# One queue's loads split over two queues, with new orders on all engines, in a fused linear-attention and GEGLU block

## The chip, the cores and the metric

The kernel runs on one core of a Trainium2 chip. The metric is the device time of one execution in microseconds (us); three runs of the kernel before gave 193.61, 193.75 and 194.16, the median being 193.75. All profile rows below come from one profiled execution of that kernel. Its engines are TensorE (PE for matmuls, PEld for weight loads), VectorE (DVE), ScalarE (ACT), GpSimd (POOL) and SyncE (SP). In the profile a "q" behind a name (SPq, ACTq) is that engine's sequencer, which issues DMAs.

## The reference, cut to what matters

Everything is bfloat16, with 2048 rows of 448 features.

```python
x = A_x                                            # [1, 2048, 448]
h = x + attn(layernorm(x))                         # wqkv [448, 1344], wo [448, 448]
#   q, k, v = split(layernorm(x) @ wqkv); 16 heads of 28
#   phi(t) = where(t > 0, t + 1, exp(t)) + 1e-6
#   kv = phi(k)^T v; z = sum over rows of phi(k)
#   o = phi(q) kv / (phi(q) z + 1e-6); attn = o @ wo
g = layernorm(h) @ w_gate                          # [448, 1792]
u = layernorm(h) @ w_up                            # [448, 1792]
h2 = h + (gelu_tanh(g) * u) @ w_down               # w_down [1792, 448]
```

## The kernel before, in words

The rows are cut into 16 tiles of 128, `t` = 0 to 15. A small recorder (`_Graph`) collects 866 tasks with a number and a name each. The engines do not run them in the order in which they were recorded: `ORDERS` holds, for each of PE, ACT, DVE, POOL and SP, the list of task numbers in the order in which that engine issues them. Each engine runs its list strictly in order, and waits on semaphores for results of other engines. A task that waits holds up all that stands behind it on its engine.

The names that the text uses are these.

- Loads: `dx0`, `dx1`, `dx2`, `dx4`, `dx8`, `dx12` (L360) bring x of tile 0, tile 1, tiles 2 and 3, and then four tiles each. `dwq` and `dwk` bring 384 rows of the Q and K weights (L353), `dwq_t` and `dwk_t` the last 64 rows (L356); after the change they are called `dw0`, `dw0_t`, `dw1`, `dw1_t`. `dwg0`, `dwu0` bring columns 0 to 767 of the MLP's gate and up weights, `dwg1`, `dwu1` the rest (L507 to L511). `dwd` brings w_down (L609).
- First layer norm, per tile: `bnst1_t`, `bnag1_t` (DVE, L413, L414), `ln1_t`, `rstd1_t` (ACT, L420, L422). For tiles 0 to 3 `normD_t` (DVE, L435) normalises, PE transposes in two halves `tr0_t`, `tr1_t` (L443), and ACT and DVE copy the halves out (`evxA_t`, `evxD_t`). For tiles 4 to 15 `normP_t` (POOL, L453) normalises and a transposing DMA `xT_t` on SP's queue (L455) turns the tile.
- Projections: `k_t` and `q_t` are four matmuls each (L469). After `k_t` come `ek_t` (ACT), `ck_t` and `pk_t` (DVE), and the sums over rows `pt4_t`, or `pt1_t` and `pt3_t` for later tiles (PE, L488). After `q_t` come `eq_t` and `rq_t` (ACT).
- Middle: `evpD_3`, `z1`, `z0` take the sums out of PSUM; `kv`, `kvm` and `w2_c` fold the value and output weights into one matrix; `evwA_c`, `evwD_c` copy it to SBUF, and `dws0`, `dws1` (SP) copy it between partition halves. For each pair `p` of tiles `cqP_p`, `aqP_p` (DVE), `t1p_t` (POOL), `drP_p`, `rdP_p`, `pnP_p` (DVE) and `deP_p` (ACT) make the normalised q; pairs 0 and 1 have their own forms (`aq_t`, `dr_t`, `deA_t`, `rd_t`, `pn_t`). A transposing DMA `oT_p` (SP, L605) turns it, and `outA_p`, `outB_p` (PE, L627, L628) multiply by the folded matrix. `hr_t` (DVE) adds x.
- Second layer norm: `bnst2_t`, `bnag2_t`; for tiles 0 and 1 `nhD_t` and `wr64_t` (DVE), the PE transposes `trh_t` (L654), and `evhA_0`, `evhD_1`. For the other tiles `negm2`, `vpe2`, `pow2`, `nhP_t` (POOL), `wrap_t` (DVE) and a transposing DMA `hT_t` (SP, L665).
- MLP: five chunks of 2, 2, 4, 4 and 4 tiles. `gu2_v` (two tiles, `v` = 0 to 13) and `gu4_v` (four tiles, `v` = 14 to 55) are the gate and up matmuls (L726, L728). `ge0_v`, `ge1_v` (ACT, L746) apply GELU, `hm0_v`, `hm1_v` (DVE, L748) multiply. Two PSUM bank pairs alternate, so number `v + 2` waits for the `hm` of number `v`. `tbl2` loads ScalarE's GELU table before the first `ge`. `downA_p`, `downB_p` (L696) multiply a pair by w_down, `fo448_t` (DVE, L702) adds h, and `do_t` (SP, L703) stores.

Before, all loads except `dx1`, `dwq_t` and `dwk_t` stand in SP's queue, beside its transposing DMAs; those three stand in ACT's.

Of the kernel before, what the change touches and what calls it, by code (L numbers as in the profile page):

```python
# [12 lines left out]


ORDERS = (
# [33 lines left out]
)  # L49
HOLD = {  # L50
    32: (31,), 35: (34,), 66: (36,), 102: (101,), 127: (126,), 166: (165,), 188: (187,), 214: (213,), 294: (292,),
    305: (302,), 323: (302,), 362: (360,), 388: (387,), 498: (378,), 631: (630,), 707: (704,), 745: (744,), 786:
    (672,), 837: (836,), 864: (863,),
}


# [173 lines left out]
def bass_sequential_preLN__linear_attn_block__glu_gated_geglu__prompt_kernel(  # L230
    nc, A_x, A_wqkv, A_wo, B_x, B_w_gate, B_w_up, B_w_down, out
):
    S, D, FF, H, DH = 2048, 448, 1792, 16, 28
# [14 lines left out]
    G = _Graph()  # L248
    es = ExitStack()
    with es:  # L250
        block = es.enter_context(nc.Block())

        def sb(name, shape, dt):
            return es.enter_context(nc.sbuf_tensor(name, shape, dt))
# [4 lines left out]
        wqk_sb = sb("wqk_sb", [128, 4, 2 * D], BF16)  # L259
        wv_sb = sb("wv_sb", [128, 4, D], BF16)  # L260
        wo_sb = sb("wo_sb", [GW, NG, D], BF16)
        wgu_sb = sb("wgu_sb", [128, NK, FF], BF16)
        wd_sb = sb("wd_sb", [128, NJ, D], BF16)
# [41 lines left out]
        def bufs(name, n):  # L305
            return [_Buf("%s%d" % (name, i)) for i in range(n)]
# [5 lines left out]
        b_wq, b_wk, b_wv = bufs("wq", 2), bufs("wk", 2), bufs("wv", 2)  # L312
        b_wpad = bufs("wpad", 2)
        b_wo, b_wg, b_wu, b_wd = _Buf("wo"), bufs("wg", 2), bufs("wu", 2), _Buf("wd")
# [15 lines left out]
        A_, B_ = slice(0, 64), slice(64, 128)  # L330
# [14 lines left out]
        def dma(q, out_ap, in_ap, w, name, r=(), after=()):  # L345
            t_ = G.add(q, lambda e: e.dma_start(out_ap, in_ap), r=r, w=w, name=name, kind="dma", after=list(after) + last[q])
            last[q] = [t_]
            return t_
# [4 lines left out]
        def dma_w3(q, dst, c0, c1, b, name):  # L353
            return dma(q, dst[:, 0:3, c0 % (2 * D):c0 % (2 * D) + c1 - c0], A_wqkv[0:384, c0:c1].rearrange("(k p) n -> p k n", p=128), [b[0]], name)

        def dma_w1(q, dst, c0, c1, b, name):  # L356
            return dma(q, dst[A_, 3, c0 % (2 * D):c0 % (2 * D) + c1 - c0], A_wqkv[384:448, c0:c1], [b[1]], name)


        def dma_x(q, a, b):  # L360
            return dma(q, x_sb[:, a:b, :], xv[:, a:b, :], b_x[a:b], "dx%d" % a)
# [2 lines left out]
            op("dve", lambda e, dst=dst: e.memset(dst[B_, 3, :], 0.0), [], [b], nm_)  # L364
        dma_x("sp", 0, 1)
        dma_x("act", 1, 2)
        dma_w3("sp", wqk_sb, 0, D, b_wq, "dwq")
        dma_w1("act", wqk_sb, 0, D, b_wq, "dwq_t")
        dma_x("sp", 2, 4)
        dma_w3("sp", wqk_sb, D, 2 * D, b_wk, "dwk")  # L370
        tx1 = dma_w1("act", wqk_sb, D, 2 * D, b_wk, "dwk_t")
        dma_x("sp", 4, 8)
        dma_x("sp", 8, 12)
        dma_x("sp", 12, 16)
# [83 lines left out]
        eks = []  # L458
# [48 lines left out]
        xts = [t for t in G.all if t.name.startswith("xT_")]  # L507
        for i in range(2):
            cs = slice(0, FC) if i == 0 else slice(FC, FF)
            dma("sp", wgu_sb[A_, :, cs], B_w_gate[:, cs].rearrange("(k p) n -> p k n", p=64), [b_wg[i]], "dwg%d" % i, after=xts[-1:])  # L510
            dma("sp", wgu_sb[B_, :, cs], B_w_up[:, cs].rearrange("(k p) n -> p k n", p=64), [b_wu[i]], "dwu%d" % i, after=xts[-1:])  # L511


        op("act", lambda e: e.activation(zbc[B_, :], ps[B_, BK_PT[3], 0:D], AF.Identity), [b_ps[BK_PT[3]]], [b_z[1]], "z1")
# [43 lines left out]
        def a2_pair(p):  # L558
# [3 lines left out]
            if p < 2:  # L562
# [3 lines left out]
                for t in (a, a + 1):  # L566
                    n = t % 2
                    eng = "dve" if t in T1_DVE else "pool"
                    op(eng, lambda e, t=t, n=n: e.tensor_tensor(t1[:, n, :], pq[:, t, :], zbc[:, :], ALU.mult), [b_pq[t]] + b_z, [b_t1[n]], "t1%s_%d" % (eng[0], t))
                for t in (a, a + 1):  # L570
                    n, i = t % 2, t % 4
# [8 lines left out]
            else:  # L580
                i, b2 = 2 * (p % 2), slice(a, a + 2)
# [24 lines left out]
                      r=b_pqn[i2], w=b_pqnT[i2], name="oT_%d" % p, kind="dma")  # L606

            if p == 1:
                dma("sp", wd_sb[:, :, :], B_w_down.rearrange("(j p) n -> p j n", p=128), [b_wd], "dwd", after=[G.all[-1]])  # L609

            if p == 0:
                for n in range(2):
# [139 lines left out]
        for nt in B1_CHUNKS:  # L752
            while done < min(P, (t0 + HR) // 2):
                a2_pair(done)
                done += 1
                if tbl2 is None:
                    tbl2 = G.add("act", lambda e: e.preload_act_table(AF.Gelu_apprx_tanh), name="tbl2", kind="nosync", after=exps)
            gu_chunk(t0, nt)
            for t in range(t0, t0 + nt, 2):
                if t < T - 2:  # L760
                    b2_pair(t // 2)
                else:
                    b2_tile(t)
                    b2_tile(t + 1)
            t0 += nt
# [52 lines left out]
```

## Time and profile before

| what | value |
|---|---|
| median of three runs | 193.75 us |
| profiled execution, its own time | 193.84 us |
| its span on the core | 191.9 us |
| outside the span | 1.94 us |
| PE busy | 185.7 us (97%) |
| DVE busy | 128.4 us (67%) |
| ACT busy | 75.2 us (39%) |
| POOL busy | 50.7 us (26%) |
| granted TensorE clock | 1.00 of full speed throughout |

The span runs from the first to the last record of the program on the core. "Busy" is the time in which an engine executes; issuing a DMA is not counted as busy. Idle time of PE is listed with the instruction that came after it and with what released that instruction.

### The profile page before, as it was taken

How to read it: one execution, taken by the hardware profiler on the slowest of the kernel's cores; microseconds unless marked ns; L12 is line 12 of the kernel's file. 1: busy time of each engine (PE TensorE's matmuls, PEld its weight loads, DVE VectorE, ACT ScalarE, POOL GpSimd, SP SyncE). 2: the span in 40 equal slices, each digit the busy share in tenths (PEclk: the TensorE clock that was granted, in tenths of full speed). 3: DMA queues.
4: the chain of work that ended last, by engine and by line, in shares of the span. 5: the costliest groups of instructions: out<-in, count | busy, mean ns of one | idle time of the engine just before them, and what ended most of it. 6: DMA issues, size and time to landing. Idle time of an engine off the chain costs nothing.

```text
span 191.9 us, 4456 instructions
## 1 busy us (share of the span) xinstructions
PE 185.7 (97%) x1813; PEld 107.3 (56%) x1813; DVE 128.4 (67%) x328; ACT 75.2 (39%) x220; POOL 50.7 (26%) x91
## 2 busy tenths in 40 slices
PE   7899999999899999999999999999998999999994
PEld 7454445655488677886455445444553445455454
DVE  3799879899799998899993863544723244415223
ACT  3689534699954222335132132432320233411200
POOL 6066730525503478235028000006300000000000
DMA  6985647999295505930221520000193000000025
GB/s 171 377 214 76 106 84 168 222 218 192 55 267 135 96 3 101 149 66 3 48 48 35 108 54 0 0 3 2 35 143 67 3 0 0 27 0 24 3 90 173
DMA packets 35077, 17.11 MB, mean 89 GB/s; under 512 B 26865, under 2 KB 33649, under 8 KB 35057
## 3 DMA queue, kind: packets, MB, share of 16 engines
q1 hardware_dynamic: 34752, 16.60, 40.9%
q8 instruction: 14, 0.23, 0.6%
q10 hardware_dynamic: 304, 0.23, 0.4%
q14 instruction: 7, 0.05, 0.1%
HBM read 8.26 MB, written 1.84 MB: 53 GB/s over the span
## 4 chain that ended last, share of the span: by engine, by line
PE 79%; DVE 11%; DMA 4%; ACT 3%; POOL 0%; SPq 0%; issue 0%
PE ps L728 38%; PE ps L696 19%; PE ps L726 7%; PE ps L469 4%; PE ps L488 3%; PE ps L678 3%; PE ps L627 3%; DMA x_sb<-in_A_x_dram 2%; DVE st L413 2%; PE ps L628 2%; DMA xnT<-xnn 2%; DVE pqn L576 1%; DVE den L572 1%; ACT e L480 1%; DVE x_sb L633 1%; DVE w L553 1%
## 5 line engine op out<-in xcount | busy, mean ns | idle before, releaser
L726 PE MATMUL ps<-hnT,wgu_sb 64*128 64x512 bf16 (+1 forms) x490 | 88.8, 333 | 0.7 <-DVE x_sb L702 0.7
L728 PE MATMUL ps<-hnT,wgu_sb 64*128 64x512 bf16 (+1 forms) x490 | 89.0, 333 | 0.0
L746 ACT ACTIVATE gl<-ps 128x256 bf16<-128x256 f32 x112 | 36.4, 383 | 81.8 <-PE ps L726 78.2
L748 DVE TENSOR_TENSOR hh<-ps,gl 128x256 bf16<-128x256 f32 x112 | 42.4, 416 | 38.6 <-ACT gl L746 38.4
L728 PEld LDWEIGHTS ps<-hnT,wgu_sb 64*128 64x128 bf16 x490 | 44.8, 94 | 31.2 <-DVE hh L748 4.6
L726 PEld LDWEIGHTS ps<-hnT,wgu_sb 64*128 64x128 bf16 x490 | 45.0, 94 | 6.3 <-DMA hnT<-hn 1.2
L696 PE MATMUL ps<-wd_sb,hh 64*128 64x448 bf16 x392 | 41.4, 349 | 0.0
L696 PEld LDWEIGHTS ps<-wd_sb,hh 64*128 64x128 bf16 x392 | 21.8, 94 | 15.8 <-issue 0.4
L469 PE MATMUL ps<-wqk_sb,xnT 128*128 128x448 bf16 x128 | 28.2, 355 | 1.0 <-DMA xnT<-xnn 0.4
L413 DVE BATCH_NORM_STATS2 st<-x_sb 128x6 f32<-128x448 bf16 x32 | 19.3, 615 | 3.2 <-DMA x_sb<-in_A_x_dram 3.1
L469 PEld LDWEIGHTS ps<-wqk_sb,xnT 128*128 128x128 bf16 x128 | 11.9, 98 | 12.7 <-DMA xnT<-xnn 1.3
L585 POOL TENSOR_TENSOR t<-pq,zbc 128x448 f32<-128x448 bf16 x12 | 13.0, 1104 | 19.6 <-DVE pq L583 18.1
L488 PE MATMUL ps<-pk,xnn 128*128 128x448 bf16 x64 | 13.9, 353 | 0.0
L627 PE MATMUL ps<-w,pqnT 64*128 64x448 bf16 x49 | 11.5, 349 | 0.8 <-DVE hn L647 0.8
L702 DVE TENSOR_TENSOR x_sb<-ps,x_sb 128x448 bf16<-128x448 f32 x14 | 8.4, 618 | 5.3 <-PE ps L696 5.3
L480 ACT ACTIVATE e<-ps 128x448 bf16<-128x448 f32 x16 | 8.6, 538 | 5.3 <-PE ps L469 5.1
L417 POOL TENSOR_SCALAR nm<-mv 128x1 f32<-128x1 f32 (+1 forms) x19 | 4.0, 218 | 24.3 <-DVE mv L414 24.0
L662 POOL TENSOR_SCALAR hn<-x_sb,nm,rs 128x448 bf16<-128x448 bf16 x14 | 10.3, 745 | 0.5
L628 PE MATMUL ps<-pt_sb,pqnT 64*128 64x448 bf16 x42 | 10.2, 350 | 0.0
L633 DVE TENSOR_TENSOR x_sb<-ps,x_sb 128x448 bf16<-128x448 f32 x16 | 9.7, 614 | 0.8 <-PE ps L628 0.8
L482 DVE SCALAR_TENSOR_TENSOR pk<-ps,e 128x448 bf16<-128x448 f32 x16 | 9.9, 619 | 0.2
L453 POOL TENSOR_SCALAR xnn<-x_sb,nm,rs 128x448 bf16<-128x448 bf16 x12 | 8.9, 743 | 3.5 <-ACT rs L422 2.9
(83 smaller groups left out, 155.5 us busy)
## 6 DMA issues: line engine op xcount, KB each, us to landing
out_dram<-x_sb SPq DMA_DIRECT2D x15, 112.0 KB, 1.8
wd_sb<-in_B_w_down_dram SPq DMA_DIRECT2D x1, 1568.0 KB, 8.0
x_sb<-in_A_x_dram SPq DMA_DIRECT2D x3, 448.0 KB, 6.3
wgu_sb<-in_B_w_gate_dram SPq DMA_DIRECT2D x1, 896.0 KB, 12.2
wgu_sb<-in_B_w_up_dram SPq DMA_DIRECT2D x1, 896.0 KB, 16.5
wqk_sb<-in_A_wqkv_dram SPq DMA_DIRECT2D x2, 336.0 KB, 4.4
wgu_sb<-in_B_w_gate_dram SPq DMA_DIRECT2D x1, 672.0 KB, 6.1
wgu_sb<-in_B_w_up_dram SPq DMA_DIRECT2D x1, 672.0 KB, 8.6
```

The costliest lines, as they stand in the source:

```text
L413: op("dve", lambda e: e.bn_stats(st[:, t, :], src_ap), [b_src], [b_st[t]], "bnst%s_%d" % (tag, t))
L469: ins = e.matmul(ps[:, bk, 0:D], xnT[:, t, k, :], wqk_sb[:, k, c0:c0 + D], start=(k == 0), stop=(k == 3))
L488: ins = e.matmul(ps[:, BK_PT[c], 0:D], xnn[:, t % XN_R, c * 128:(c + 1) * 128], pk[:, ip, :], start=(t == 0), stop=(t == T - 1))
L585: op("pool", lambda e, n=n: e.tensor_tensor(t1[:, n, :], pq[:, a + n, :], zbc[:, :], ALU.mult), [b_pq[a + n]] + b_z, [b_t1[n]], "t1p_%d" % ...
L627: e.matmul(ps[:, BK_OUT[0], 0:D], pqnT[ra, i2, sg // 2, :], w2[ra, sg // 2, :], start=(sg == 0), stop=(sg == 5))
L628: ins = e.matmul(ps[:, BK_OUT[1], 0:D], pqnT[rb, i2, 3 + (sg + 1) // 2, :], (w2 if sg == 6 else w2s)[rb, sg // 2, :], start=(sg == 0), sto ...
L633: op("dve", lambda e, t=t, bo=bo: e.tensor_tensor(x_sb[:, t, :], ps[:, bo, 0:D], x_sb[:, t, :], ALU.add), [b_ps[bo], b_x[t]], [b_x[t]], "h ...
L696: ins = e.matmul(ps[:, BK_O[n], 0:D], hh[rows, j, sl[n]], wd_sb[rows, j, :], start=(half == 0 and j == 0), stop=(half == 1 and j == NJ - 1))
L726: first = e.matmul(psG[:, jj * N:(jj + 1) * N], wgu_sb[A_, k, j * 128:(j + 1) * 128], hnT[A_, ka_, c0:c0 + N], start=(k == 0), stop=(k == ...
L728: ins = e.matmul(psU[:, jj * N:(jj + 1) * N], wgu_sb[B_, k, j * 128:(j + 1) * 128], hnT[B_, kb_, c0:c0 + N], start=(k == 0), stop=(k == NK ...
L746: G.add("act", lambda e, gi=gi, cs_=cs_, psG=psG: e.activation(gl[:, gi, cs_], psG[:, cs_], AF.Gelu_apprx_tanh), r=[b_ps[BK_G[i]]], w=[b_g ...
L748: op("dve", lambda e, dst=dst, srcU=srcU, srcL=srcL: e.tensor_tensor(dst, srcU, srcL, ALU.mult), [b_ps[BK_U[i]], b_glh], [b_ar[j_][t % HR] ...
```

## The change

Two things are changed. First, the queues of some loads. `dx2` (tiles 2 and 3, "three and four" when counted from one) moves ahead of the weights in SP's queue. The 384 rows of Q weights go to ACT's queue, and so do the four gate and up loads and w_down; the condition that put the gate and up loads behind the last `xT` becomes one that puts them behind `ek_11`, and the condition on w_down is dropped. Second, the five lists in `ORDERS` are new, and so is `HOLD` (which of several waits of an instruction is put first). The work itself, its tile sizes, buffers and PSUM banks stay as they were.

```diff
-    "29 35 37 66 46 44 69 53 55 74 79 62 64 82 87 73 90 78 102 86 119 114 94 129 106 165 141 118 133 153 145 177"
...
+    "29 37 35 44 46 66 69 53 74 64 55 79 62 82 87 73 90 78 119 102 86 114 94 129 106 141 165 118 133 153 145 177"
...
         dma_x("sp", 0, 1)
         dma_x("act", 1, 2)
-        dma_w3("sp", wqk_sb, 0, D, b_wq, "dwq")
-        dma_w1("act", wqk_sb, 0, D, b_wq, "dwq_t")
         dma_x("sp", 2, 4)
-        dma_w3("sp", wqk_sb, D, 2 * D, b_wk, "dwk")
-        tx1 = dma_w1("act", wqk_sb, D, 2 * D, b_wk, "dwk_t")
+        dma_w3("act", wqk_sb, 0, D, b_wq, "dw0")
+        dma_w1("act", wqk_sb, 0, D, b_wq, "dw0_t")
+        tx1 = dma_w1("act", wqk_sb, D, 2 * D, b_wk, "dw1_t")
+        dma_w3("sp", wqk_sb, D, 2 * D, b_wk, "dw1")
         dma_x("sp", 4, 8)
...
-            dma("sp", wgu_sb[A_, :, cs], B_w_gate[:, cs].rearrange("(k p) n -> p k n", p=64), [b_wg[i]], "dwg%d" % i, after=xts[-1:])
-            dma("sp", wgu_sb[B_, :, cs], B_w_up[:, cs].rearrange("(k p) n -> p k n", p=64), [b_wu[i]], "dwu%d" % i, after=xts[-1:])
+            dma("act", wgu_sb[A_, :, cs], B_w_gate[:, cs].rearrange("(k p) n -> p k n", p=64), [b_wg[i]], "dwg%d" % i, after=eks[11:12])
+            dma("act", wgu_sb[B_, :, cs], B_w_up[:, cs].rearrange("(k p) n -> p k n", p=64), [b_wu[i]], "dwu%d" % i, after=eks[11:12])
...
-                dma("sp", wd_sb[:, :, :], B_w_down.rearrange("(j p) n -> p j n", p=128), [b_wd], "dwd", after=[G.all[-1]])
+                dma("act", wd_sb[:, :, :], B_w_down.rearrange("(j p) n -> p j n", p=128), [b_wd], "dwd")
```

Read by names, the parts of the new orders that the text uses are these.

| engine | before | after |
|---|---|---|
| SP, start | dx0 dwq dx2 dwk dx4 | dx0 dx2 dw1 dx4 |
| ACT, start | dx1 dwq_t dwk_t tbl1 | dx1 dw0 dw0_t dw1_t tbl1 |
| PE, start | tr0_0 tr1_0 q_0 tr1_1 tr0_1 k_0 | tr1_0 tr0_0 tr0_1 tr1_1 q_0 k_0 |
| SP, first transposes | xT_6 xT_9 xT_7 xT_8 | xT_6 xT_7 xT_9 xT_8 |
| PE | k_6 pt4_4 k_9 k_7 | k_6 pt4_4 k_7 k_9 |
| ACT | ek_11 ek_13 ek_12 ek_14 | ek_11 dwg0 ek_13 dwu0 dwg1 ek_12 ek_14 |
| PE | k_15 ... pt1_15 ... q_4 | q_4 k_15 ... pt1_15 |
| ACT | deA_1 deA_0 ... deA_2 | deA_0 dwu1 deA_1 deA_2 |
| DVE | evpD_3 z0 aq_1 t1d_0 | aq_1 evpD_3 z0 t1d_0 |
| DVE | nhD_1 cqP_3 wr64_1 wr64_0 rdP_2 | nhD_1 rdP_2 wr64_0 wr64_1 ... cqP_3 |
| ACT | evhA_0 eq_14 rq_12 eq_12 tbl2 | evhA_0 rq_15 eq_13 rq_14 eq_14 rq_13 tbl2 |
| ACT | ge0_1 ge1_2 | ge0_1 deP_3 dwd ge0_2 |
| SP | dws0 dws1 oT_1 oT_2 dwd oT_3 hT_2 hT_3 | dws0 dws1 oT_1 oT_2 oT_3 hT_3 hT_2 |
| PE | outB_3 downA_0 gu2_7 gu2_8 | outB_3 gu2_7 gu2_8 downA_0 |
| POOL | nhP_4 ... nhP_7 t1p_11 t1p_10 | t1p_11 t1p_10 ... nhP_5 nhP_4 ... nhP_7 |
| SP, last four tiles | hT_14 do_3 hT_15 do_4 hT_12 hT_13 | hT_13 do_3 hT_15 hT_14 hT_12 |
| PE, end | downA_6 down448_14 downB_6 down224_15 (two) | downA_6 down224_15 downB_6 down448_14 down224_15 |

More of the change, by code (lines that the diff above doesn't have):

```diff
@@ L15 @@
 ORDERS = (
[33 rows of a table removed]
[34 rows of a table added]
 )
 HOLD = {
-    32: (31,), 35: (34,), 66: (36,), 102: (101,), 127: (126,), 166: (165,), 188: (187,), 214: (213,), 294: (292,),
-    305: (302,), 323: (302,), 362: (360,), 388: (387,), 498: (378,), 631: (630,), 707: (704,), 745: (744,), 786:
-    (672,), 837: (836,), 864: (863,),
+    66: (36,), 139: (138,), 165: (164,), 175: (174,), 305: (298,), 362: (360,), 388: (387,), 431: (283,), 498:
+    (375,), 521: (518,), 531: (528,), 571: (570,), 581: (580,), 591: (590,), 621: (620,), 699: (497,), 755:
+    (754,), 767: (764,), 849: (846,), 864: (863,),
 }
```

65 rows, old and new, of the table ORDERS are left out of this document.

## Prediction

> **What bounds the kernel now.** I read the page's busy shares first, then stretches of the span, the waits of PE's weight loads, the chain, and the DMA views.
>
> ```profile
> PE 185.7 (97%) x1813; PEld 107.3 (56%) x1813; DVE 128.4 (67%) x328; ACT 75.2 (39%) x220; POOL 50.7 (26%) x91
> ```
>
> TensorE sets the time, and the change removes none of its 1813 matmuls. Only its idle time can be won, or added to. Stretches of the span (start:end, length, PE, PEld, DVE, ACT, POOL busy, clock, DMA share, GB/s) show where that idle time is:
>
> ```profile
> 0.00:7.90 7.90, 6.23 (x52) 5.09 (x53) 3.71 (x11) 3.05 (x9) 3.06 (x10) 1.00 0.78 250
> ...
> 34.10:49.00 14.90, 14.14 (x92) 7.71 (x90) 14.36 (x36) 13.40 (x35) 6.26 (x8) 1.00 1.05 202
> 49.00:52.20 3.20, 3.15 (x34) 1.77 (x36) 2.35 (x4) 2.81 (x7) 2.39 (x2) 1.00 0.08 15
> 52.20:145.50 93.30, 93.30 (x1094) 57.22 (x1090) 67.74 (x169) 30.09 (x92) 27.47 (x44) 1.00 0.38 71
> 145.50:146.30 0.80, 0.08 (x3) 0.04 (x4) 0.70 (x2) 0.00 (x0) 0.00 (x0) 1.00 0.19 39
> ```
>
> From 52.2 to 145.5 PE never stops, so a stall put there is lost in full. Between 34.1 and 49.0 VectorE is busy for 14.36 of 14.90 us: it sets that stretch. The waits of the weight loads (total, times, longest) name what PE lacks:
>
> ```profile
> PEld ps L469 <- DMA xnT<-xnn: 1.3, 2, 0.8
> PEld ps L627 <- DMA pqnT<-pqn: 1.3, 1, 1.3
> PEld ps L726 <- DMA hnT<-hn: 1.2, 1, 1.2
> ```
>
> All are transposing DMAs of SP's queue. In starts of matmuls the losses are 0.18 and 0.57 us at `k_6` and `k_7` (18.38, 21.23), 0.98 at `outA_1` (49.05) and 0.88 at 146.27. The chain shows the first loss of all, tiles 2 and 3 of x, and the second:
>
> ```profile
> 1.71 4.70 DMA x_sb<-in_A_x_dram
> ...
> 6.43 0.63 DVE st L413
> ...
> 17.77 3.41 DMA xnT<-xnn
> ...
> 21.23 0.93 PE ps L469 x4
> ```
>
> A DMA's time runs from issue to landing. In the stretch 43 to 46 us the issues read:
>
> ```profile
> pt_sb<-w SPq DMA_DIRECT2D x1, 168.0 KB, 5.4
> pqnT<-pqn SPq DMA_TRANSPOSE x1, 5.2
> ```
>
> That `oT_1` landed at 49.0; the seven of its kind have a median of 2.9. It stood behind the MLP weights in one queue (the last issued at 30.9, 16.5 to land).
>
> **Start.** `dx2` is issued at 1.24 instead of 1.71, without 336 KB of Q weights ahead of it. Its landing is bounded by the same flight of 4.70 (5.94, from 6.41) and by about 4.1 (the first tile lands at 3.3; 224 KB more at some 300 GB/s). The Q weights now share the engines with it, so I take 5.1. VectorE is free of tile 1 at 5.15 (`bnag1_1` 5.06, then 0.09), so `bnst1_2` goes from 6.43 to about 5.2. But `k_0` needs the K weights, which landed at 7.3 with the same bytes to move ahead of them. Thus `k_0` goes from 7.92 to 7.45: 0.45 us. ScalarE issues one more load before `tbl1` (2.43): some 0.5 us, the table ends at 4.2, just where `ln1_0` (4.19) needs it. Cost 0, or 0.1 if the issue is slow.
>
> **Projections.** All first transposes begin 0.5 us earlier and `xT_7` goes ahead of `xT_9`, so the losses of 0.75 at `k_6`, `k_7` should go. VectorE, never idle from 7.9 to 21.2 (13.30 of 13.30), is late next; I leave 0.3 for waits on `pk_4` to `pk_6`, so 0.45 is won.
>
> Three gate and up issues now stand in ScalarE's list between `ek_11` and `ek_12`. At 0.63 to 0.69 each that is 2.0 us, beside six operations of 0.43: 4.6 us against 5.3 us of matmuls from `k_13` to `k_15`. Cost 0, but `ek_13` and `pk_13` wait behind them if ScalarE is late. `dwg0` goes out near 26.5, while `xT_15` (27.6 before) is near 26.6: they collide. Before, `dwg0` needed over 1.5 us from issue to any dense traffic, so I take 0.2, up to 1.0.
>
> **Middle.** From `evpD_3` (34.13) to the end of `wr64_0` (49.00) VectorE's strip is 14.87 us. `aq_1` (0.39) and `cqP_3` (0.35) leave it, `rdP_2` (0.26) enters: 14.4. `dwu1` (0.69) stands between `deA_0` and `deA_1` on ScalarE, with `rd_1` and `pn_1` waiting behind; the new order uses them 2 us later, so 0, at most 0.7. The strip starts after `pt1_15`, which now has `q_4` (0.76) ahead of it: 34.13 + 0.76 - 0.45 - 0.45 + 0.2 = 34.2. So `wr64_0` ends at 48.6 to 49.3. `outA_1` no longer waits for `oT_1`, as weights and transposes are in different queues, so `trh_0` follows `wr64_0` directly instead of at 49.92. The first MLP matmul (52.14) comes 1.2 us earlier; bounds 0.4 and 1.8 (all waits gone).
>
> Here the Trainium skill speaks against the change: "DMA: Bandwidth & Descriptors", section "Issuing engines are not separate DMA queues", says that issuing from several engines saves only issue time. By it `oT_1` would still be late; that is the second rival below. No run yet decides it.
>
> **Into the MLP.** Between `evhA_0` and `tbl2` ScalarE has five `eq`/`rq` instead of three: 0.86 us. `ge` of `gu2_0`, then `hm1_0`, move back as much, and `gu2_2` had about 0.4 us of cover after the last `hm` (55.68 to 55.95, plus latency). A new loss of 0.4, from 0 to 0.6.
>
> `dwd` moves from 52.02 to behind `deP_3`, about 4.3 us after the first MLP matmul. Its issue (0.58) stands before `ge0_2`, where ScalarE idled 1.42: 0. It is needed by `downA_0`, now about 16 us after that matmul, and took 8.0 to land: covered by 4. But its 8 us now lie on `oT_3`, `hT_3`, `hT_2`, which it preceded before. Alone these need 2.9 to 3.1 each; their packets move 229 KB at about 215 GB/s, 1.07 us each. Bounds: nothing (they slip between the weights), or all three behind the whole load: 4.3 + 8.0 + 3.2 = 15.5 against a need by `gu2_7` at 65.48 - 52.14 = 13.3, 2.2 us. `outA_3` has 1.6 us of cover for `oT_3`. I take 0.6, nearer to nothing: `oT_3` has most of its cover used before `outA_3` waits, and the weights' traffic starts thin, as `dwg0`'s did.
>
> **Late MLP.** The stall at 146.27 came from SP's queue (start, length, count):
>
> ```profile
> 137.13 1.22 SPq L665 DMA_TRANSPOSE hnT<-hn  x1
> 138.40 0.58 SPq L703 DMA_DIRECT2D out_dram<-x_sb  x1
> 139.02 1.23 SPq L665 DMA_TRANSPOSE hnT<-hn  x1
> 140.29 0.58 SPq L703 DMA_DIRECT2D out_dram<-x_sb  x1
> 140.92 3.62 SPq L665 DMA_TRANSPOSE hnT<-hn  x2
> ```
>
> One store (0.63 with its gap) leaves, and the first transpose follows the first `wrap` (136.2) instead of the third: 0.9 earlier. Together 1.5, over 0.88, so the stall goes: 0.88 won, 0.5 if a transpose is again 1 us late. POOL's two `t1p` (1.04 each) now precede `nhP_4` to `nhP_7`; `hT_5` should still land over 1 us before its matmul: 0, or 1.0 if that cover is gone. Stores move to the end of SP's list, 0.48 apart; the last still follows `fo224_15` (189.37): 0, or 0.5 if one is in its way. All other reorderings keep two matmul groups between a bank's use and reuse: 0.
>
> **Sum**, on the profiled execution (193.84; 0.09 over the median): 193.84 - 1.2 + 0.4 + 0.6 - 0.88 = 192.76, or 192.7 against the median. What this kernel can tell from no change is about 0.3%, 0.6 us.
>
> **Rivals.** *Two queues collide* (slower). Weights from ScalarE's queue alternate with the transposes on the same DMA engines, so that a transpose takes as long as the weights beside it. Price: 2.2 instead of 0.6 at `gu2_7`, and 0.8 more at `xT_15`: 192.7 + 1.6 + 0.8 = 195.1. It decides once the collisions cost 1.7 us (0.6 + 1.1). For it: the two tiles of x that were issued at 0.8 on two queues landed after 2.5 and 2.7, so neither queue goes first. Against: `oT_3` has 1.6 us of cover. The skill ("DMA: Bandwidth & Descriptors", "Queues, rings and completion order") states that each DMA engine goes round-robin between its queues, a packet at a time; the trace agrees with its 2.5 and 2.7.
>
> *VectorE hides the start.* If the strip and the dense stretch before it set the first MLP matmul, it comes only 0.2 earlier: with half of the costs 193.84 - 0.2 + 0.3 + 0.3 - 0.88 = 193.4, no measurable change. For it: VectorE's 14.36 of 14.90. This is also the result if `oT_1` stays late on its own queue.
>
> *All cover holds.* 193.75 - 1.8 - 0.88 = 191.1. For it: each cost has cover by its nearest row; against: that all do.
>
> That the change does not do what it says is not a rival of weight: the loads do move.
>
> **Numbers.** Forecast 0.40 (0.35 faster, 0.05 same), all cover 0.09 (faster), hidden 0.16 (0.03 faster, 0.10 same, 0.03 slower), collision 0.35 (0.01 same, 0.34 slower). So faster 0.47, same 0.16, slower 0.37. The forecast's own range is 191.9 to 193.5, from its bounds. The 8-in-10 range reaches nearly to full cover and just over the collision: 191.4 to 195.2.
>
> **What would show it.** Right: the first MLP matmul near 51; no PEld wait on pqnT at L627; `bnst1_2` near 5.2; no gap before the last chunk's first matmul. Collision: PEld waits at L726 or L627 on hnT or pqnT between 58 and 68, or on xnT near 30, with transposes at 4 us or more from issue to landing. Hidden: first MLP matmul at 51.9 or later. The forecast is wrong if PE waits over 1 us on VectorE or ScalarE in a place not named here.

## The result, and the profile after

The kernel after takes 196.25 us (median) against 193.75 us before: a ratio of 1.014, with a 95% interval of 1.011 to 1.017. It is slower by 1.4%. Of six runs five took 195.91 to 197.51 us and give the ratio; the sixth took 201.24 at a lower granted clock and is left out of it. Its profiled execution took 196.05 us with a span of 194.3, against 193.84 and 191.9 before; the forecast was 192.7.

The first line of the page (busy time, share of the span and instructions of each engine) shows that the work of TensorE is what it was:

```profile
PE 185.2 (95%) x1813; PEld 115.4 (59%) x1813; DVE 127.9 (66%) x328; ACT 76.1 (39%) x220; POOL 49.6 (26%) x91
```

PE is busy for nearly the same time (185.2 us against 185.7) and its share fell from 97% to 95%, so the 2.4 us by which the span grew are new idle time. Cut into stretches where the trace's matmuls stop (columns as in the prediction: PE, PEld, DVE, ACT, POOL busy, clock, DMA share, GB/s), the span shows two holes:

```profile
0.00:7.25 7.25, 5.52 (x52) 4.58 (x53) 4.52 (x15) 3.48 (x10) 2.68 (x10) 1.00 0.75 245
30.60:34.00 3.40, 1.26 (x8) 0.51 (x6) 1.71 (x4) 1.22 (x3) 0.00 (x0) 1.00 1.23 188
36.76:50.90 14.14, 14.14 (x96) 7.62 (x94) 13.97 (x35) 12.19 (x32) 5.52 (x5) 1.00 0.75 158
...
63.90:66.20 2.30, 0.33 (x7) 0.10 (x4) 2.30 (x7) 0.66 (x2) 0.97 (x1) 1.00 1.12 104
66.20:148.90 82.70, 82.53 (x911) 56.16 (x912) 54.83 (x139) 24.54 (x76) 21.88 (x36) 1.00 0.32 52
```

`k_0` starts at the end of the first row. The second row holds a stop ahead of `k_15`. The third is VectorE's strip from `evpD_3` to `wr64_0`: 14.14 us, with PE now busy in all of it. The fourth is a stop ahead of `outA_3`, inside the stretch where PE never stopped before. Taken by starts of matmuls, as in the prediction, the stops are 2.30 and 2.13 us. The chain of waits (start, length, what) names what ended each of them; these are its lines around the first and the second:

```profile
26.30 0.91 POOL xnn L454
...
27.24 6.34 DMA xnT<-xnn
33.59 0.14 issue
33.73 0.92 PE ps L470 x4
```

```profile
59.55 6.44 DMA pqnT<-pqn
66.00 0.14 issue
66.13 0.35 PE ps L628
```

Both are transposing DMAs on SP's queue, `xT_15` and `oT_3`. Before, they took 2.4 and 2.9 us from issue to landing; now 6.34 and 6.44. What moved in the meantime can be read from the DMA queues. q10 carries what ScalarE issued (the loads), q1 what SP issued (`xT_15` has packets of 256 bytes). The columns are packets, MB and the share of 16 engines' time. First the stretch 28.5 to 30.5 us, then 31 to 32.5 us:

```profile
q10 hardware_dynamic: 270, 0.41, 84.5%
```

```profile
q1 hardware_dynamic: 516, 0.13, 93.3%
q10 hardware_dynamic: 98, 0.13, 65.8%
```

`xT_15` was issued from 27.24 to 28.43. In two microseconds after that not one of its packets moved; `dwg0`, issued at 26.33 on the other queue, had the engines to itself. `xT_15` moved once `dwg0` had nearly gone: by 31 us 372 of the 448 packets of `dwg0` had moved. `oT_3`, issued from 59.55 to 60.78, shows the same behind `dwd`: from 58 to 62 us only q10 moved.

```profile
q10 hardware_dynamic: 1365, 1.22, 94.9%
```

So the places and the culprits are those of the rival *two queues collide*. Its 2.2 us for `dwd` was the price of waiting for the whole load, and 2.13 were measured. For `xT_15` it had 1.0 us (0.2 and 0.8 more); there, too, the wait was for nearly the whole load, 2.30.

### The profile page after: what moved, and what is told of

Same layout as the page of the kernel before. It is cut to its first block, busy times and chain, and to the rows that moved or that the text cites. A ratio compares the mean times of both kernels' runs of the same rounds, so it can differ in the third digit from the quotient of the medians.

```text
span 194.3 us, 4464 instructions
## 1 busy us (share of the span) xinstructions
PE 185.2 (95%) x1813; PEld 115.4 (59%) x1813; DVE 127.9 (66%) x328; ACT 76.1 (39%) x220; POOL 49.6 (26%) x91
## 3 DMA queue, kind: packets, MB, share of 16 engines
q1 hardware_dynamic: 30688, 11.44, 29.5%
## 4 chain that ended last, share of the span: by engine, by line
PE 80%; DMA 11%; DVE 4%; issue 1%; ACT 1%; ACTq 1%; POOL 1%
PE ps L729 31%; PE ps L697 17%; PE ps L727 9%; PE ps L470 9%; DMA xnT<-xnn 5%; PE ps L489 4%; DMA pqnT<-pqn 3%; DMA wqk_sb<-in_A_wqkv_dram 3%; PE ps L679 3%; PE ps L628 3%; PE ps L629 2%; DVE hh L749 1%; PE ps L618 1%; ACTq L347 1%; PE ps L548 1%
## 5 line engine op out<-in xcount | busy, mean ns | idle before, releaser
L727 PEld LDWEIGHTS ps<-hnT,wgu_sb 64*128 64x128 bf16 x490 | 45.4, 94 | 2.3
L697 PEld LDWEIGHTS ps<-wd_sb,hh 64*128 64x128 bf16 x392 | 23.0, 94 | 14.3 <-issue 0.2
L470 PEld LDWEIGHTS ps<-wqk_sb,xnT 128*128 128x128 bf16 x128 | 11.9, 98 | 14.4 <-DVE pk L483 2.5
L586 POOL TENSOR_TENSOR t<-pq,zbc 128x448 f32<-128x448 bf16 x12 | 12.3, 1040 | 28.3 <-DVE pq L584 25.9
L489 PEld LDWEIGHTS ps<-pk,xnn 128*128 128x128 bf16 x64 | 6.3, 98 | 5.8 <-DVE pk L483 0.2
```

The lines of the kernel that those rows point to most:

```text
L470: ins = e.matmul(ps[:, bk, 0:D], xnT[:, t, k, :], wqk_sb[:, k, c0:c0 + D], start=(k == 0), stop=(k == 3))
L489: ins = e.matmul(ps[:, BK_PT[c], 0:D], xnn[:, t % XN_R, c * 128:(c + 1) * 128], pk[:, ip, :], start=(t == 0), stop=(t == T - 1))
L586: op("pool", lambda e, n=n: e.tensor_tensor(t1[:, n, :], pq[:, a + n, :], zbc[:, :], ALU.mult), [b_pq[a + n]] + b_z, [b_t1[n]], "t1p_%d" % ...
L697: ins = e.matmul(ps[:, BK_O[n], 0:D], hh[rows, j, sl[n]], wd_sb[rows, j, :], start=(half == 0 and j == 0), stop=(half == 1 and j == NJ - 1))
L727: first = e.matmul(psG[:, jj * N:(jj + 1) * N], wgu_sb[A_, k, j * 128:(j + 1) * 128], hnT[A_, ka_, c0:c0 + N], start=(k == 0), stop=(k == ...
```

## The experiments

All times below are for the kernel after with one edit, unless another base is named. Each was taken beside the kernel before on the same chip, and the ratios are to that. The median of the kernel before was 193.11 to 193.23 us there, some 0.5 below the 193.75 of the result, so times are best compared with each other and not with 196.25. "One run" marks a time that was measured once. "Gap" is PE's lost time between two starts of matmuls.

The main theory, *order of issue*: DMAs of both queues are served in the order in which they were issued. The rivals: *shares* (the queues alternate packet by packet, the prediction's own mechanism), *turns* (whole loads alternate), *yields* (a transpose gives way to any plain load).

**A second load ahead of `xT_15`.** In ScalarE's order:

```diff
-ek_11 dwg0 ek_13 dwu0 dwg1 ek_12
+ek_11 dwg0 dwu0 ek_13 dwg1 ek_12
```

> Only the place of dwu0 changes: ScalarE issues it right behind dwg0 (about 27.0), ahead of xT_15 (27.24); in the kernel after it came behind xT_15 (27.85). Theory, order of issue: DMAs of both queues are served in the order in which they were issued, so xT_15 waits for both loads. dwu0's traffic takes about 3.9 us more (landings of dwg0 and dwu0 in the kernel after: 33.08 and 36.99), so xT_15 lands near 37.3 instead of 33.59, k_15 waits some 6.0 instead of 2.3 us, and the time is about 199.7. Rival, turns: the queues are served by turns, one whole DMA each; xT_15 comes behind dwg0 alone as before, lands near 33.6, gap 2.3, time 196.0. Rival, shares (the prediction's own mechanism): the queues alternate packet by packet; one more load behind the first in ScalarE's queue takes no larger share, so also near 33.6 and 196.0.

Measured: 204.92 us (one run). PE's waits (total, times, longest) and the stretches around `k_15` (its start is 39.97):

```profile
PE ps L471 <- DMA xnT<-xnn: 8.5, 2, 8.0
```

```profile
38.00:39.90 1.90, 0.00 (x0) 0.00 (x0) 0.00 (x0) 0.00 (x0) 0.00 (x0) 0.50 0.70 138
39.90:42.00 2.10, 2.04 (x6) 0.87 (x7) 0.00 (x0) 0.35 (x1) 0.00 (x0) 0.50 0.40 98
42.00:44.00 2.00, 2.00 (x6) 0.73 (x5) 1.20 (x3) 0.63 (x2) 0.00 (x0) 0.50 0.03 6
```

`k_15` waited 8.2 us, so *turns* falls: `xT_15` came behind both loads. *Shares* as stated falls with it. Two things went beyond the expected 6.0. `dwg1` was issued from 28.18 to 28.78, inside the issue of `xT_15` (27.58 to 28.95), and the two then went packet for packet. The queues from 36 to 38 us:

```profile
q10 hardware_dynamic: 128, 0.26, 95.7%
q1 hardware_dynamic: 127, 0.03, 14.2%
```

And the clock granted to TensorE (the column before the DMA share) was 0.50 after the stop: until 45.4 us a matmul of 448 columns took 0.374 us instead of 0.19. The span is 8.9 us longer than that of the kernel after. The longer stop is 5.9 of them, and 5.4 us at half speed lose another 2.7, by an estimate from these rows.

**The loads behind `xT_15`.**

```diff
-ek_11 dwg0 ek_13 dwu0 dwg1 ek_12
+ek_11 ek_13 dwg0 dwu0 dwg1 ek_12
```

> dwg0, dwu0 and dwg1 are issued behind ek_13, so dwg0 near 27.85, 0.6 us after xT_15 (27.24); all stay on ScalarE's queue, dwu1 stays where it is. Theory, order of issue: xT_15 lands after its usual 2.4 to 2.7 us (29.7 to 30.0), k_15 starts near 31.4 without a gap, and 2.3 us are won there. But everything behind then comes 2.3 earlier while the loads come a little later: dwu1 lands near 47.5, oT_1 (issued near 43.5) waits for it and lands near 49.5, and outA_1, wanted near 47.8, gives back 1.5 to 2.2. Time 195.3 (194.8 to 196.0). Rival, shares: dwg0 and xT_15 overlap for over 1 us of traffic, xT_15 needs 4 us or more, k_15 keeps a gap near 0 (its cover is 4.2 us from issue), and oT_1 is slowed little: 193.8. Rival, transposes yield to any plain load: xT_15 waits for dwg0 again, lands near 34.5, gap 3, time 196.7.

Measured: 194.24 us, ratio 1.006 (1.004 to 1.008). `xT_15` was issued at 27.64 and landed after 2.4 us; `k_15` had no gap. The queues from 28.5 to 29.5 us and from 29.9 to 31.5 us:

```profile
q1 hardware_dynamic: 511, 0.13, 62.8%
```

```profile
q10 hardware_dynamic: 198, 0.30, 80.1%
```

`dwg0`, issued 0.6 us behind `xT_15`, began when the transpose was through. That contradicts *yields*. As expected, part of the gain was given back later:

```profile
PE ps L629 <- DMA pqnT<-pqn: 2.2, 2, 1.6
```

`oT_1` (issued at 43.88) landed at 48.71, behind `dwu1`, which landed at 47.13, and `outA_1` had a gap of 0.72. It was less than the 1.5 to 2.2 expected, as `oT_1` landed 0.8 earlier than the 49.5 put down for it. `oT_3`, still behind `dwd`, cost 1.76.

**`dwd` ahead of the GELU table.** In ScalarE's order, from behind `deP_3`:

```diff
-rq_15 eq_13 rq_14 ... deP_3 dwd ge0_2
+rq_15 dwd eq_13 rq_14 ... deP_3 ge0_2
```

> Only the place of dwd in ScalarE's order changes: behind rq_15, issued near 52.4, just behind oT_2 (52.02), instead of 56.64. Theory, order of issue: dwd lands near 59.6, before oT_3 (issued 59.55) has any traffic, so oT_3 lands after its usual 2.9 us (62.5), the gap of 2.13 at outA_3 goes, and the time is 194.0 (193.8 to 194.4, the upper end if the issue delays the first GELUs). oT_2 keeps its landing. Rival: the gap at outA_3 only stands in for one that is due anyway behind it (hT_3, hT_2 and VectorE's work for gu2_7), so that gu2_7 then waits over 1 us, and the time stays over 195.

Measured: 200.45 us, ratio 1.037 (1.033 to 1.041), against an expected 194.0. The expectation assumed an issue at 52.4. The timelines of ScalarE's and of SyncE's sequencer (start, length, what) show another order:

```profile
50.60 0.38 ACTq L348 DMA_DIRECT2D wd_sb<-in_B_w_down_dram  x1
```

```profile
51.05 1.22 SPq L607 DMA_TRANSPOSE pqnT<-pqn  x1
```

The load does not wait until the activation ahead of it in the list has begun: `rq_15` began to execute at 51.41. So the list is the order in which ScalarE's sequencer issues, and not the order in which the work begins. Here `dwd` was ahead of `oT_2` by 0.45 us, `oT_2` took 8.7 us, and the stop moved to `outA_2`:

```profile
PEld ps L629 <- DMA pqnT<-pqn: 4.6, 1, 4.6
```

```profile
60.00:62.00 2.00, 2.00 (x16) 1.02 (x14) 0.00 (x0) 0.00 (x0) 0.00 (x0) 0.50 0.50 94
62.00:64.00 2.00, 2.00 (x23) 1.35 (x21) 0.00 (x0) 0.00 (x0) 0.00 (x0) 0.50 0.00 0
```

`outA_3` had no gap. The expected time was missed, but the wait went where the theory puts it, to the transpose that now stood behind the load. Again the clock was 0.50 after the stop of 4.48.

The same edit was made again, with `dwd` behind `rq_14` and one more condition, so that it is surely behind `oT_2`:

```diff
+        G.dep(by["dwd"], [by["evhD_1"]])
```

> Only dwd is moved in the kernel after, as in wd_early, but it is issued only once evhD_1 is done and so surely behind oT_2, whose issue begins near 52.0. Theory, order of issue: oT_2 lands after its usual 2.9 to 3.2 us, dwd (issued near 52.9) lands near 60.3, oT_3 (59.55) near 62.6, and both gaps, 4.48 at outA_2 in wd_early and 2.13 at outA_3 in the kernel after, are gone: 194.0 (193.8 to 194.4). Rival, transposes wait for any plain load under way or about to start: oT_2 waits again, over 198.

Measured: 192.96 us (one run). `oT_2` took 3.0 us and `oT_3` 2.9, neither `outA_2` nor `outA_3` had a gap, and `k_15` still had one of 1.44 behind `dwg0`. The time is 1.0 less than the 194.0 expected; that smaller gap is 0.86 of it, and the other chip can be a part. The gap at `outA_3` was a real loss, and no later stop stood behind it.

**`dwd` between `oT_3` and `hT_3`.**

```diff
-ge0_1 deP_3 dwd ge0_2 ge1_2 ge0_3 ge1_3 ge1_4
+ge0_1 deP_3 ge0_2 ge1_2 ge0_3 ge1_3 dwd ge1_4
```

> Only the place of dwd in ScalarE's order changes: behind ge1_3, issued near 60.8, after oT_3 (59.55) and just ahead of hT_3 (61.10) and hT_2. Theory, order of issue: oT_3 lands after its usual 2.9 us (62.5) and the gap at outA_3 goes, though the same load is under way beside it; hT_3 and hT_2 wait for the whole load (landing near 68), land near 69.5 and 70.5, and gu2_7, wanted near 66.9, waits some 3.7 us. Time 197.6. Rival, shares: oT_3 is a little slower, hT_3 and hT_2 take 4 to 5 us, land at 65 to 66, and gu2_7 does not wait: 194.0 to 194.5.

Measured: 198.71 us (one run). The DMA issues from 60 us on, with their time to landing, in which the first two rows are `dwd`, and `hT_3` and `hT_2`:

```profile
wd_sb<-in_B_w_down_dram ACTq DMA_DIRECT2D x1, 1568.0 KB, 9.1
hnT<-hn SPq DMA_TRANSPOSE x2, 8.4
```

`oT_3`, issued at 59.04, 0.94 ahead of `dwd`, landed after 3.02 us; `hT_3`, issued 0.6 behind it, after 8.7. `gu2_7` waited 3.64 (expected 3.7). The transposes are the same kind on the same queue; only their place in the order of issue differs. *Shares* had 194.0 to 194.5. The 1.1 us over the expected 197.6 fits the clock, which was 0.50 from 71.18 to 74.59 us: 3.4 us at half speed lose 1.7, and the gap at `k_15` was 0.8 smaller than in the kernel after.

**All five loads back on SP, the rest of the change kept.** This undoes the queue change of the MLP loads alone and puts them back in their places of the kernel before:

```diff
-            dma("act", wgu_sb[A_, ...], ..., "dwg%d" % i, after=eks[11:12])
-            dma("act", wgu_sb[B_, ...], ..., "dwu%d" % i, after=eks[11:12])
+            dma("sp", wgu_sb[A_, ...], ..., "dwg%d" % i)
+            dma("sp", wgu_sb[B_, ...], ..., "dwu%d" % i)
...
-                dma("act", wd_sb[:, :, :], ..., "dwd")
+                dma("sp", wd_sb[:, :, :], ..., "dwd")
```

> The kernel after, with its start and its orders, but all five MLP loads back on SyncE's queue at the places of the kernel before: dwg0, dwu0, dwg1, dwu1 behind xT_15, dwd between oT_2 and oT_3. Theory, order of issue: it is the time of issue and not the queue that counts. xT_15 lands after 2.4 us (2.3 won), oT_3 after 2.9 (2.1 won); dwu1 lands near 47, so oT_1 (issued near 43.7) waits for it and outA_1 has a gap of 0.7 to 1.3: 196.05 - 2.3 - 2.1 + 1.0 = 192.6, ratio 0.994 (0.990 to 0.998). So this undoes the whole loss and shows what the rest of the change is worth. Rival, a second queue helps by itself: moving the loads back costs what the prediction had put down to it (oT_1 behind the weights, 1.2 us of the middle, and more at outA_1), and the time is 194 or over, no faster than the kernel before.

Measured: 192.45 us, ratio 0.9965 (0.994 to 0.999). `k_15` and `outA_3` had no gap, `outA_1` one of 1.05, since `oT_1` (43.57) stood behind `dwu1` and landed at 48.71. So the whole loss lies in the MLP loads, and the rest of the change is worth 0.7 us (0.3 to 1.1 by the interval). `oT_1` landed at the same 48.71 in *the loads behind `xT_15`*, with the loads on the other queue: the queue made no difference.

**`dwu1` and `dwd` behind their transposes, on ScalarE's queue.** The edit of *the loads behind `xT_15`*, and:

```diff
+        G.dep(by["dwu1"], [by["cqP_2"]])
+        G.dep(by["dwd"], [by["evhD_1"]])
```

with `dwu1` behind `rq_11` and `dwd` behind `rq_14`.

> Every MLP load is issued just behind a transpose that would otherwise wait for it, all still on ScalarE's queue: dwg0, dwu0, dwg1 behind ek_13 (as in gu_late), dwu1 behind rq_11 and not before cqP_2 is done (so behind oT_1), dwd behind rq_14 and not before evhD_1 is done (so behind oT_2). Theory, order of issue: xT_15, oT_1, oT_2 and oT_3 all land 2.4 to 3.2 us after issue, and the two gaps that gu_late's profile still had, 0.72 at outA_1 and 1.76 at outA_3, go: gu_late's ratio to before, 1.0059, less 2.5 of 193.2 us gives 0.993 (0.989 to 0.996), about 1.4 us faster than the kernel before. Rival, VectorE's strip sets the middle: outA_1's gap goes but the first MLP matmul does not come earlier, only outA_3's is won: ratio 0.997. Rival, shares: transposes that overlap the loads still take 4 us or more; ratio 1.00 or above.

Measured: 198.71 us, ratio 1.028 (1.025 to 1.031). A miss. The chain and the issues show `oT_1`:

```profile
44.40 9.26 DMA pqnT<-pqn
```

```profile
44.40 1.35 SPq L607 DMA_TRANSPOSE pqnT<-pqn  x1
```

```profile
44.62 0.60 ACTq L348 DMA_DIRECT2D wgu_sb<-in_B_w_up_dram  x1
```

`dwu1` began 0.22 behind `oT_1`, but its issue was complete at 45.22 and that of `oT_1` at 45.74. Now both were in service together. From 48 to 49.5 us the packets went one for one:

```profile
q10 hardware_dynamic: 119, 0.24, 88.0%
q1 hardware_dynamic: 118, 0.03, 16.8%
```

`outA_1` waited 5.13 us, with the half clock behind it. So "issued first" has to be sharpened. Where a load did not disturb the transpose ahead of it, the issue of the transpose had also *ended* first (`dwg0` and `xT_15` of *the loads behind `xT_15`*: 28.89 and 28.83, `dwd` and `oT_3` of *`dwd` between*: 60.36 and 60.27). Here, as with `dwg1` and `xT_15` of *a second load*, the load began later and ended earlier, and the two shared the engines.

The test of that keeps ScalarE's queue and lets `dwu1` wait a little longer:

```diff
-        G.dep(by["dwu1"], [by["cqP_2"]])
+        G.dep(by["dwu1"], [by["hr_0"]])
```

> As both_late, all MLP loads on ScalarE's queue, but dwu1 is issued only once hr_0 is done, so that its issue ends after that of oT_1 (in both_late it ended 0.52 us before). Theory, order by the end of issue: oT_1 lands after 2.5 to 3.2 us instead of 9.26, outA_1's gap of 5.13 and the half clock behind it go, and the time is that of sp_behind within 0.5 us, though the loads are on the other queue. Rival: a second queue is what lets a load disturb a transpose that was issued first; oT_1 stays at 5 us or more, outA_1 has a gap of over 2 us, and the time is over 195.

Measured: 191.89 us (one run). The issues, SyncE's and ScalarE's:

```profile
43.41 1.35 SPq L607 DMA_TRANSPOSE pqnT<-pqn  x1
```

```profile
44.82 0.60 ACTq L348 DMA_DIRECT2D wgu_sb<-in_B_w_up_dram  x1
```

1.41 us behind instead of 0.22, and `oT_1` took 3.3 us instead of 9.26; `outA_1` had no gap. The load was issued 1.2 us later on the same two queues, and the time is 6.8 us less (198.71 against 191.89, on two chips): about the stop of 5.13 and the 1.7 that 3.4 us at half clock lose by estimate.

Is it the end of the issue that decides, or a lead of some 0.6 us between the beginnings? Every undisturbed transpose of the runs had both. But in *a second load* `dwg1` began 0.60 us behind `xT_15`, as far as `dwg0` did in *the loads behind `xT_15`* (0.60) and `dwu0` in the kernel after (0.60). These two ended 0.06 and 0.03 behind the transpose and did not disturb it; `dwg1` ended 0.17 ahead of it and shared the engines with it. So the same lead came out both ways, and the order of the ends tells them apart. It is one case, and in it two loads were already ahead.

**The same with the loads on SP**, that is the kernel with all five loads on SP and `dwu1` behind `oT_1` in its list:

```diff
-dwg0 dwu0 dwg1 dwu1 dws0 dws1 oT_1 oT_2 dwd oT_3
+dwg0 dwu0 dwg1 dws0 dws1 oT_1 dwu1 oT_2 dwd oT_3
```

> As mlp_on_sp, with dwu1 moved from behind dwg1 to behind oT_1 in SyncE's list, so that its issue begins only when oT_1's has ended. Theory, order by the end of issue (a load waits for a transpose and a transpose for a load, whichever had been issued completely first, whatever the queue): dws0, dws1 and oT_1 land 2.3 to 3 us after issue, the gap of 1.05 at outA_1 goes, and the next task, trh_0, then waits for wr64_0 of VectorE, done 0.95 before trh_0's present start: 0.95 us faster than mlp_on_sp, 0.9965 less 0.0049 = 0.992 of before (0.989 to 0.995). oT_2 (issued near 48.8, with dwu1 still moving until 50) lands 1 to 2 us late, within the cover of outA_2. Rival: loads beside a transpose slow it however they are ordered, as oT_1's 9.3 us beside dwu1 in both_late might mean; then outA_1's gap is 3 us or more and the ratio 1.005 or above.

Measured: 191.37 us, ratio 0.992 (0.989 to 0.995), as expected. Its gap at `outA_1` is gone, `trh_0` waits 0.14 for VectorE, and from 52 to 146 us PE is nearly back to what it was before (93.80 us busy of 94.00):

```profile
52.00:146.00 94.00, 93.80 (x1096) 65.26 (x1093) 66.81 (x169) 30.77 (x93) 28.71 (x45) 1.00 0.39 69
```

This version is faster than both kernels, by 0.8% against before. The single run with the loads on ScalarE's queue lies 0.5 us above it.

**`dw1_t` ahead of `dx4`.** In the early loads, on the kernel just shown (a separate run of the edit on the 198.71 us kernel gave the same picture, see below):

```diff
-        tx1 = dma_w1("act", wqk_sb, D, 2 * D, b_wk, "dw1_t")
         dma_w3("sp", wqk_sb, D, 2 * D, b_wk, "dw1")
+        dma_w1("sp", wqk_sb, D, 2 * D, b_wk, "dw1_t")
```

> As sp_behind, with dw1_t on SyncE's queue ahead of dx4, as in both_late_k, where k_0's last quarter no longer waited. Theory: the stall of some 0.4 to 0.7 us in k_0 goes, dw1_t lands near 7.3: 0.4 to 0.5 us faster than sp_behind, ratio 0.989 (0.986 to 0.993). Rival: VectorE, which has no idle time from 8 to 21 us, takes the gain back before k_10, and the ratio stays that of sp_behind.

Measured: 191.76 us, ratio 0.993 (0.990 to 0.996): no gain that can be told from its base, so the rival's outcome. The step itself worked: `dw1_t` landed at 7.61, and `k_0` had no gap, where its base had 0.61. But `q_0` had one of 0.39 and `k_6` one of 0.36, which the base had not, and the base had one of 1.01 at `k_9`. Stops at these places differ from run to run (`q_0` from none to 0.95 and `k_9` from none to 1.01 in kernels that have the same loads there), and a gain of 0.4 cannot be told apart in that. Whether VectorE takes it back stays open. On the 198.71 us kernel:

> As both_late, and dw1_t (the last 64 rows of the K weights) is issued on SyncE's queue between dw1 and dx4, near 2.17 instead of behind dx4's issue at 2.31 on ScalarE's; ScalarE issues one load less before its table load. Theory, order of issue, at the start too: dw1_t lands near 7.3 instead of 8.2 to 8.8, as it no longer stands behind dx4's 448 KB, and the stall of 0.2 to 0.6 in k_0's last quarter goes: 0.4 us faster than both_late, ratio 0.991. Rival: the small loads land late for their own small packets and not for their place; k_0's stall stays and the ratio is that of both_late.

Measured: 198.26 us, ratio 1.026 (1.023 to 1.030), with `dw1_t` at 7.33 and no gap in `k_0`. The two intervals overlap, so the 0.45 us there is not shown either.

## Why the prediction was wrong

**The start** was right in its steps. `dx2` landed at 4.79 (forecast 5.1), `bnst1_2` started at 5.12 (5.2), `k_0` at 7.27 (7.45). What was missing is a row I did not price: `dw1_t`, the last 64 rows of the K weights, was issued behind `dx4`, landed at 8.20, and stopped `k_0` for 0.41 before its last quarter.

**Projections**: half right. `k_6` and `k_7` lost nothing, but `k_9` lost 0.55 to `xT_9`, so that `k_11` came 0.41 earlier, where 0.9 had been forecast together with the start. The issues of loads cost ScalarE nothing, as forecast.

**The step that failed: `xT_15` against `dwg0`**, "I take 0.2, up to 1.0". It was 2.30. The reason given, that `dwg0` needed over 1.5 us to any dense traffic, is true (few packets before 29 us) and beside the point: the transpose did not move in the thin part either. The bound of 1.0 allowed for two loads that share the engines; the runs show a wait for all of the earlier one.

**The middle**: the strip was right (14.14 us against 14.4). The number behind it seems to fit too: the first MLP matmul was 1.04 later than before, and so 1.26 earlier without the 2.30, where 1.2 was forecast. That is luck, since the reason "as weights and transposes are in different queues" is refuted. `oT_1` was early because `k_15`'s stop had given the loads 2.3 us. With that stop away and ScalarE's queue kept (*the loads behind `xT_15`*), `outA_1` lost 0.72 and the first MLP matmul started at 51.84, only 0.30 earlier than before; on SP's queue `outA_1` lost 1.05. The section "Issuing engines are not separate DMA queues" of the Trainium skill's page "DMA: Bandwidth & Descriptors" says that issuing from several engines saves only issue time. The runs agree: `oT_1` landed at 48.71 from either queue.

**Into the MLP**: the `eq` and `rq` cost 0.21 at `gu2_2` (0.4 forecast, from 0 to 0.6). **The second step that failed is `dwd`**, 0.6 with a bound of 2.2. It was 2.13, and at `outA_3`, not at `gu2_7`: `oT_3` was 3.5 us late against its 1.6 us of cover, which was named correctly. The upper bound was the case that occurred; the choice "nearer to nothing" rested on the same thin traffic.

**Late MLP**: right. No gap ahead of the last chunk's first matmul, 0.88 won, and no store in the way at the end.

With the two measured stops in the place of 0.2 and 0.6 the sum gives 192.76 - 0.8 + 2.30 + 2.13 = 196.39, against 196.05. All other terms together were off by 0.3 us. That is closer than they deserve: projections won less than forecast, and the 1.2 of the middle holds only together with the stop at `k_15`.

**The rivals**: *two queues collide* named the places and got 195.1. Its mechanism, an alternation, is only part of the truth. The Trainium skill ("DMA: Bandwidth & Descriptors", "Queues, rings and completion order") has each DMA engine go round the queues that it has work for, a packet at a time. The trace agrees where two DMAs are in service together (119 packets against 118). Where one had been issued well before, the trace shows no turns: 270 packets against none. Whether `xT_15` was then held back at the DMA engines or had not been handed to them yet, no run shows. An alternation from the issue on, as the rival had it, would have moved packets of `xT_15` from 28.5 us on.

## What to carry to other kernels

In this kernel a small DMA that an engine waits for was late by all the bytes that had been issued ahead of it, on whichever queue. That holds for the plain copies too: `dws0` and `dws1` took 4.7 to 5.5 us from issue to landing where most of `dwu1` was still ahead of them, on either queue, and 2.6 to 2.9 where `dwu1` was issued after them. Moving a big load to another engine's queue did not take it out of the way, and put it in the way, because its issue was no longer ordered against the small one. Issue each big load right behind the small transfer that would otherwise wait for it, in the same list or with an explicit condition that comes clearly later, and check the issue times of both in the trace. When a load is moved, price the wait of every short transfer that is issued before the load lands at the load's full remaining time first, and lower it only with a row that shows the two moving together.

## What the runs showed of the hardware that was not expected

- Service across the two queues followed the order of issue. A transpose issued less than 1 us behind a load took 5.5 to 8.7 us, behind two loads (and beside a third) 12.3, and just ahead of one, with its issue ended first, 2.4 to 3.3. What in the hardware keeps this order, no run shows.
- A transpose and a load that began later but whose issue ended first went packet for packet, and both became slow: `oT_1` took 9.26 and `dwu1` 9.2 us, where they took 3.3 and 7.2 with `dwu1` issued 1.2 us later.
- A stop of TensorE costs more than its length once it is long. With stops of 3.64, 4.48, 5.13 and 8.22 us the granted clock fell to 0.50 (0.374 us instead of 0.19 for a matmul of 448 columns); with 2.30 and 2.13 it stayed at 1.00. In that order of the stops it was 0.50 from 71.18 to 74.59, 57.46 to 64.29, 53.60 to 57.02 and 35.15 to 45.39 us: once, twice, once and three times 3.41 us. The first of these began 1.2 us after the stop had ended, the second 2.0 us after the last matmul ahead of the stop. The Trainium skill's page "TensorE: Matmul & The Clock Gate" ("Part 1: The HAM clock gate") gives about 3.4 us idle as the point and about as long busy until the clock is back. The runs agree with the 3.4 us as the step; that all of it must be idle they do not bear out, as the fall after 2.0 us shows.
- ScalarE's sequencer issued a DMA at 50.60 that stood in its list behind an activation which began at 51.41. A place in the list did not fix the time of the load's issue; a condition did: with the one on `evhD_1`, which ended at 52.06, the issue began at 52.09.
